# The tail's scores and the products with U, moved to a step's head between weighted values and main scores

## The chip, the cores and the metric

The kernel runs on one core of one Trainium2 chip. The metric is the device time of the program in microseconds; the time before is 1704.91 us, the median of three runs (1704.02, 1704.91, 1705.40). Everything is in fp32.

## The reference

Two blocks follow one another, over 8 batches of 8 heads, a sequence of 576 and a head dimension of 64.

```python
# attention in which each row keeps its 32 largest scores
scores = (1/8) * q @ k.T                       # 576 x 576 for each of 64 heads
kth = np.partition(scores, -32, axis=-1)[..., -32:-31]
scores = np.where(scores >= kth, scores, -1e9)
attn = exp(scores - max) / (sum + 1e-9)
x = (attn @ v), heads side by side             # (8, 576, 512)
# mixer: U is 576 x 32, V 32 x 576, w_ch1 512 x 2048, w_ch2 2048 x 512
h = x.T @ U @ V
u = x + h.T
out = u + np.maximum(u @ w_ch1, 0) @ w_ch2
```

## The kernel before

**Groups and tiles.** Two heads form a group g; there are 32 groups, four to a batch. The 576 rows of a group are four main tiles of 128 rows (both heads, scores of 2 x 576 columns) and a tail of 64 rows, in which both heads lie on top of each other: head 0 on partitions 0 to 63, head 1 on 64 to 127. The first four groups (ALONE) run a stage of their own, with five steps each. From group 4 on, a group takes four steps, and the fourth holds the last main tile and the tail together; these two-tile steps are where the change acts.

**What a tile goes through.** `scores` (product at L334) multiplies q and k into PSUM tiles `sc` of two banks each, of which two exist (pool ps_s). A main tile takes two `sc` tiles and fills 288 of the 512 columns of each bank; the tail takes one. ScalarE copies them to SBUF: L360 (into Ssb, main tiles of the later groups), L351 (into Stail, the tail). `fold` and `split` (L397, L399, L400, GpSimd and VectorE) split the scores into an upper and a lower half; VectorE finds the 32 largest with MAX8 and MATCH_REPLACE8 (L450 to L485). ScalarE and GpSimd mask the rest (L511, L514, L515), and ScalarE takes the exponential (L404). VectorE's 32 x 32 transposes (L541, into y), a write to DRAM (away) and a read back (L556, into PT, issued on ScalarE's queue) turn the weights around; tails and the earliest groups use TensorE for this (L577, L582). `values` multiplies with v into O (L602 for a tail, L615 and L618 for a main tile), three steps after the tile's own step; ScalarE copies O to XT (L627), or scales it into x (L610) for the tail.

**After a group.** `mixed` is a generator that a step's `fill` calls advance piece by piece. It transposes XT (L641), copies it to x (L645) and scales it on GpSimd (L646), waits for a number of `fill` calls, then multiplies with U (pT, L652), copies to Tb (L660) and computes two pieces of u transposed (up, L664 and L666, copied to uT at L674). After a batch's fourth group, its `mlp` joins the list of fillers.

**Fillers.** `mlp` yields after each matmul (mm, L701 with w1 and L719 with w2). `fill` first advances `mixed`, and then hands out as much of the first filler as a share worked out from the total allows; where the list is empty, the share is dropped, and that work is done after the attention is over. `tick` counts mm matmuls and starts, 12 of them later, the transposes and stores of finished results (L764, L766, and out_dram on SP's queue).

**Order.** All five engines are scheduled by hand: each engine executes its instructions in the order in which the program issues them. In a step n of the second stage:

```python
fill()
weighted(n - 3)                 # O of the step three back, tail first
for tile_ in tiles(n + 1):      # scores of the next step's main tile
    if tile_[1] < NT:
        scores(*tile_)
    fold(*tile_)
turn(); fill(); turn() ...
```

and at the very end of the step, after most of its fillers:

```python
if len(tiles(n + 2)) > 1:
    scores(*tiles(n + 2)[1])    # the tail's scores, two steps ahead
fill()
```

pT comes where the wait of five `fill` calls after L646 ends, in the middle of the step after the tail's O. PSUM has three pools of two buffers each: `sc`, `tp` (transposes, O, pT, up), and `mm`.

Of the kernel before, what the change touches and what calls it, by code (L numbers as in the profile page):

```python
# [8 lines left out]
F32 = mybir.dt.float32  # L9
# [17 lines left out]
def kernel(  # L27
# [28 lines left out]
    nc = tc.nc  # L56
    B, H, S, D = q.shape
    P = 128
# [4 lines left out]
    NT, TAIL = 4, 64  # L63
    MAIN = NT * P
    HALF = S // 2
    assert S == MAIN + TAIL and D == 64 and H % 2 == 0 and C == 512 and TOPK % 8 == 0
    NPAIR = H // 2
# [15 lines left out]
    attn = ctx.enter_context(tc.tile_pool(name="attn", bufs=2))  # L83
# [42 lines left out]
    def rows(t):  # L126
        return P if t < NT else TAIL

    def cols(t):
        return slice(t * P, t * P + rows(t))  # L130
# [4 lines left out]
    def half(h):  # L135
        return slice(h * D, (h + 1) * D)
# [97 lines left out]
    raw, qkTs, S2s, uTs, XTs, dens = {}, {}, {}, {}, {}, {}  # L234
    probs, PTs, folds, fronts_of = {}, {}, {}, {}
# [54 lines left out]
    def blocked(g):  # L290

        return g > NPAIR
# [23 lines left out]
            copy(qkT[:, i, 0:MAIN], tp.rearrange("p t n -> p (t n)"))  # L318
            yield

    def scores(g, t):

        qkT = qkTs[g]
        if t == NT and g >= NPAIR:
            S2 = attn.tile([P, S], F32, tag="Stail", name="Stail", bufs=1)
        else:
            S2 = attn.tile([P, 2 * (S + TAIL)], F32, tag="Ssb", name="Ssb", bufs=4)
        n = 2 if t < NT else 1  # L330
        probs[g, t] = S2
        S2s[g, t] = S2[:, 0 : n * S].rearrange("p (c n) -> p c n", c=n)
        def product(out, h, lo, hi):
            nc.tensor.matmul(  # L334
                out,
                lhsT=qkT[half(h), 0, cols(t)],
                rhs=qkT[half(h), 1, lo:hi],
                start=True,
                stop=True,
            )  # L340

        if t == NT:
            sc = ps_s.tile([P, 2, 512], F32, tag="sc", name="sc")
            for i in range(2):
                for h in range(2):
                    lo = i * HALF + (TAIL if h and blocked(g) else 0)
                    hi = min(lo + HALF, S)
                    product(sc[half(h), i, 0 : hi - lo], h, lo, hi)
                    if hi - lo < HALF:
                        product(sc[half(h), i, hi - lo : HALF], h, 0, TAIL)  # L350
            nc.scalar.copy(S2[:, 0:S].rearrange("p (i n) -> p i n", i=2), sc[:, :, 0:HALF])  # L351
            return
        scs = [ps_s.tile([P, 2, 512], F32, tag="sc", name="sc") for _ in range(2)]
        for i, sc in enumerate(scs):
            for h in range(2):
                part = 1 - i if h and blocked(g) else i
                product(sc[:, h, 0:HALF], h, part * HALF, (part + 1) * HALF)
        if blocked(g):
            for i, sc in enumerate(scs):
                nc.scalar.copy(ends_of(S2, i), sc[:, :, 0:HALF])  # L360
            fronts_of[g, t] = scs[0][:, :, 0:HALF]
            return

        main = S2.rearrange("p (h n) -> p h n", h=2)
        last = S2[:, MAIN : MAIN + 2 * TAIL].rearrange("p (h n) -> p h n", h=2)
        copy = nc.vector.tensor_copy if g + t == 0 else nc.scalar.copy
        copy(main[:, :, 0:HALF], scs[0][:, :, 0:HALF])  # L367
        nc.scalar.copy(main[:, :, HALF:MAIN], scs[1][:, :, 0 : MAIN - HALF])
        nc.scalar.copy(last, scs[1][:, :, MAIN - HALF : HALF])

    def ends_of(S2, i):

        parts = S2[:, 0 : 4 * HALF].rearrange("p (a n) -> p a n", a=4)
        return parts[:, 1:3] if i else parts[:, 0:4:3]
# [217 lines left out]
    def values(g, t):  # L592

        PT = PTs.pop((g, t))
        va, vd, vt = (a[g % NV] for a in (vas, vds, vts))
        O = ps_t.tile([P, P], F32, tag="tp", name="O")
        if t == NT:
            den, x = dens[g], xs[g % 2]
            if g not in inverted:
                inverse(g, 2 * NT if g == NPAIR - 1 else 0, 2 * NT + 1)  # L600
            for j in range(NT + 1):
                nc.tensor.matmul(  # L602
                    O,
                    lhsT=PT[:, j],
                    rhs=va[:, :, j, :] if j < NT else vt,
                    start=(j == 0),
                    stop=(j == NT),
                )
            for h in range(2):
                nc.scalar.mul(x[half(h), NT, half(h)], O[half(h), half(h)], den[half(h), 2 * NT :])  # L610
            return
        if shared(g, t):
            PT = PT.rearrange("p c n -> p (c n)")
            PT = PT.rearrange("p (a c j) -> p c a j", a=4, j=BLK)
        nc.tensor.matmul(O, lhsT=vd, rhs=PT[:, 2 * NT], start=True, stop=False)  # L615
        for j in range(NT):
            for h in range(2):
                nc.tensor.matmul(  # L618
                    O[half(h)],
                    lhsT=va[:, h, j, :],  # L620
                    rhs=PT[:, NT * h + j],
                    start=False,
                    stop=(j == NT - 1),
                )
        if t == 0:
            XTs[g] = attn.tile([P, MAIN], F32, tag="XT", name="XT", bufs=1)
        nc.scalar.copy(XTs[g][:, cols(t)], O)  # L627


    def mixed(g, wait, lag=0):  # L630

        for _ in range(lag):
            yield
        b, gi = divmod(g, NPAIR)
        if gi == 0:
            uTs[b] = mlpp.tile([P, NC, S], F32, tag="uT", name="uT")
        XT, den = XTs.pop(g), dens[g]
        X = xs[g % 2]
        tp = ps_t.tile([P, NT, P], F32, tag="tp", name="tp")
        for t in range(NT):  # L640
            nc.tensor.transpose(tp[:, t, :], XT[:, cols(t)], ident)  # L641
        X4 = X[:, 0:NT, :].rearrange("p t (h d) -> p t h d", h=2)
        tp4 = tp.rearrange("p t (h d) -> p t h d", h=2)
        den4 = den[:, 0 : 2 * NT].rearrange("p (t h) -> p t h ()", h=2).to_broadcast([P, NT, 2, D])
        nc.scalar.copy(X4, tp4)  # L645
        nc.gpsimd.tensor_tensor(X4, X4, den4, ALU.mult)  # L646
        for _ in range(wait):
            yield
        pT = ps_t.tile([P, P], F32, tag="tp", name="pT")
        for t in range(NT + 1):  # L650
            i = t % NT * R
            nc.tensor.matmul(  # L652
                pT[i : i + R, :],
                lhsT=U[:, t, :],
                rhs=X[:, t, :],
                start=(t < NT),
                stop=(0 < t),
            )
        Tb = mlpp.tile([P, P], F32, tag="Tb", name="Tb")
        nc.scalar.copy(Tb, pT)  # L660
        yield
        for chunks, (lo, hi) in zip(PARTS, SPAN):
            up = ps_t.tile([P, WIDE], F32, tag="tp", name="up")
            nc.tensor.matmul(up[:, 0 : hi - lo], lhsT=Tb, rhs=V[:, lo:hi], start=True, stop=False)  # L664
            for t in chunks:
                nc.tensor.matmul(  # L666
                    up[:, OFF[t] - lo : OFF[t] - lo + rows(t)],
                    lhsT=X[:, t, :],
                    rhs=ident if t < NT else ident2,
                    is_transpose=True if t < NT else None,  # L670
                    start=False,
                    stop=(t == chunks[-1]),
                )
            nc.scalar.copy(uTs[b][:, gi, lo:hi], up[:, 0 : hi - lo])  # L674
            yield
        if gi == NPAIR - 1:
            fillers.append(mlp(b))

    posts, ticks = [], 0

    def later(wait, job):

# [102 lines left out]
    STEPS = len(steps)  # L785
# [5 lines left out]
    fillers, mixing, due = [], [], 0.0  # L791
# [21 lines left out]
    def tiles(n):  # L813

        return steps[n] if 0 <= n < STEPS else []

    def weighted(m):

        for g, t in reversed(tiles(m)):
            values(g, t)  # L820
        if tiles(m)[-1][1] == NT:
            mixing.append(mixed(g, 5, 1 if m < STEPS - 1 else 0))

    def turn():

# [10 lines left out]
    t = 0  # L836
    for _ in prep(0):
        pass
    scores(0, 0)
    turning = ready = iter(())  # L840
    fronts = {}
    for n in range(STEPS + 2):
        if n < STEPS:
            g, t = steps[n][0]
# [6 lines left out]
        else:  # L851
            t = NT
# [71 lines left out]
        fill()  # L924
        if ALONE <= n - 3 <= STEPS - 3:
            weighted(n - 3)
        for tile_ in tiles(n + 1):
            if tile_[1] < NT:
                scores(*tile_)
            fold(*tile_)  # L930
        turn()
        fill()
# [37 lines left out]
            next_params(1)  # L970
        next(here, None)
        fill()
        if len(tiles(n + 2)) > 1:
            scores(*tiles(n + 2)[1])
        fill()
    while mixing or fillers:
        fill()
# [33 lines left out]
```

## Time and profile before

| | us |
|---|---|
| median of three runs | 1704.91 |
| lowest, highest | 1704.02, 1705.40 |
| the profiled execution | 1704.56 |
| its span, first to last instruction | 1702.7 |
| TensorE matmuls busy (PE) | 1606.2 |
| VectorE busy (DVE) | 1495.9 |
| ScalarE busy (ACT) | 993.5 |
| GpSimd busy (POOL) | 900.5 |

The profile shows one execution; times are counted from its first instruction. PE is TensorE's matmuls, PEld its weight loads. Matmuls overlap, and the busy time of PE counts a matmul until its results are out, so the start of the following one tells more than its length. Every fp32 matmul leaves two records. The chain of waits follows the work back from the last instruction: each piece in it was waited for by the next. A wait is put down to the instruction that came last. The first stage takes until about 233 us (the first O of group 4); the last O starts at 1557 us, and from then on only the last batch's mlp and its stores are left.

### The profile page before, as it was taken

How to read it: one execution, taken by the hardware profiler on the slowest of the kernel's cores; microseconds unless marked ns; L12 is line 12 of the kernel's file. 1: busy time of each engine (PE TensorE's matmuls, PEld its weight loads, DVE VectorE, ACT ScalarE, POOL GpSimd, SP SyncE). 2: the span in 40 equal slices, each digit the busy share in tenths (PEclk: the TensorE clock that was granted, in tenths of full speed). 3: DMA queues.
4: the chain of work that ended last, by engine and by line, in shares of the span. 5: the costliest groups of instructions: out<-in, count | busy, mean ns of one | idle time of the engine just before them, and what ended most of it. 6: DMA issues, size and time to landing. Idle time of an engine off the chain costs nothing.

```text
span 1702.7 us, 29005 instructions
## 1 busy us (share of the span) xinstructions
PE 1606.2 (94%) x9385; PEld 1210.6 (71%) x9385; DVE 1495.9 (88%) x4286; ACT 993.5 (58%) x2422; POOL 900.5 (53%) x695
## 2 busy tenths in 40 slices
PE   4566789999999999999999999999999999999999
PEld 2444556787677877788777877788777877788777
DVE  7999998999999999999999999999999999991000
ACT  4888778665556656565656556565656556563100
POOL 4778568656555555555555555555555555551000
PEclk7788899999999999999999999999999999999999
DMA  3322232255445454554544454554544454532010
GB/s 87 96 83 85 65 85 69 63 135 129 124 122 128 118 134 119 140 127 118 124 123 125 122 130 119 137 127 122 125 122 124 120 135 117 134 106 79 4 16 13
DMA packets 275832, 180.95 MB, mean 106 GB/s; under 512 B 173920, under 2 KB 260192, under 8 KB 275680
## 3 DMA queue, kind: packets, MB, share of 16 engines
q1 hardware_dynamic: 259648, 117.49, 29.8%
q10 hardware_dynamic: 16032, 61.61, 11.3%
q8 instruction: 74, 1.21, 0.3%
q14 instruction: 78, 0.64, 0.1%
HBM read 108.23 MB, written 70.78 MB: 105 GB/s over the span
## 4 chain that ended last, share of the span: by engine, by line
PE 85%; DVE 12%; ACT 1%; POOL 1%; issue 1%; DMA 0%; SPq 0%; DVEq 0%; POOLq 0%; ACTq 0%
PE mm L719 29%; PE mm L701 29%; PE sc L334 9%; PE O L618 7%; DVE m L485 5%; DVE upper L480 5%; PE up L664 2%; PE O L602 2%; DVE first L467 2%; PE O L615 1%; PE tp L577 1%; PE up L666 1%; PE pT L652 1%; PE tp L764 1%; PE tp L641 1%; DVE w L186 1%
## 5 line engine op out<-in xcount | busy, mean ns | idle before, releaser
L719 PE MATMUL mm<-hT,w 128*128 128x256 f32 (+1 forms) x2048 | 530.4, 409 | 0.0
L701 PE MATMUL mm<-uT,w 128*128 128x256 f32 (+1 forms) x2048 | 529.6, 410 | 0.0
L515 POOL TENSOR_TENSOR Ssb<-Ssb,E 128x576 f32<-128x576 f32 x243 | 339.7, 1417 | 275.7 <-ACT E L514 275.4
L701 PEld LDWEIGHTS mm<-uT,w 128*128 128x128 f32 x2048 | 379.2, 191 | 109.5 <-issue 8.4
L719 PEld LDWEIGHTS mm<-hT,w 128*128 128x128 f32 x2048 | 377.2, 190 | 104.4 <-issue 12.7
L485 DVE MAX8 m<-upper 128x8 f32<-128x304 f32 (+1 forms) x780 | 367.2, 512 | 0.7
L480 DVE MATCH_REPLACE8 upper<-m,upper 128x304 f32<-128x304 f32 (+1 forms) x520 | 259.7, 507 | 0.0
L397 POOL TENSOR_TENSOR lower<-Ssb 128x576 uint32<-128x576 uint32 x108 | 152.7, 1414 | 152.8 <-issue 100.1
L334 PE MATMUL sc<-qkT 64*128 64x288 f32 (+1 forms) x1334 | 210.2, 437 | 11.2 <-ACT Ssb L367 7.8
L404 ACT ACTIVATE Ssb<-Ssb,nmax 128x576 f32<-128x576 f32 x258 | 200.9, 780 | 18.6 <-POOL Ssb L491 9.7
L714 ACT ACTIVATE hT<-mm 128x320 f32<-128x320 f32 (+1 forms) x256 | 104.6, 409 | 181.9 <-PE mm L701 178.2
L400 POOL TENSOR_TENSOR lower<-lower,upper 128x576 uint32<-128x576 uint32 x108 | 152.7, 1414 | 100.3 <-DVE upper L399 95.2
L452 DVE MAX8 upper<-lower 128x8 f32<-128x288 f32 x432 | 172.3, 440 | 9.8 <-POOL lower L400 9.7
L514 ACT ACTIVATE E<-Ssb,least 128x576 f32<-128x576 f32 x243 | 176.2, 768 | 4.3
L334 PEld LDWEIGHTS sc<-qkT 64*128 64x128 f32 (+1 forms) x1334 | 115.6, 182 | 73.7 <-issue 29.0
L541 DVE STREAM_TRANSPOSE y<-Ssb 128x512 f32<-128x512 f32 (+1 forms) x312 | 154.8, 546 | 7.0 <-ACT Ssb L404 6.4
L360 ACT COPY Ssb<-sc 128x576 f32<-128x576 f32 x216 | 127.7, 644 | 36.6 <-PE sc L334 36.6
L618 PE MATMUL O<-PT,va 128*64 128x128 f32 x2048 | 144.5, 285 | 0.0
L731 DVE TENSOR_TENSOR oT<-uT,mm 128x320 f32<-128x320 f32 (+1 forms) x8 | 3.6, 454 | 144.6 <-PE mm L719 144.6
L618 PEld LDWEIGHTS O<-PT,va 128*64 128x64 f32 x2048 | 113.1, 140 | 16.1 <-issue 1.3
L399 DVE TENSOR_TENSOR upper<-sc,Ssb 128x576 f32<-128x576 f32 x108 | 80.3, 744 | 22.2 <-ACT Ssb L360 22.0
L480 DVE MATCH_REPLACE8 upper<-first,upper 128x304 f32<-128x304 f32 x216 | 97.7, 460 | 0.0
(111 smaller groups left out, 1893.3 us busy)
## 6 DMA issues: line engine op xcount, KB each, us to landing
away<-y SPq DMA_DIRECT2D x416, 144.0 KB, 2.5
PT<-away ACTq DMA_DIRECT2D x104, 576.0 KB, 3.8
raw<-in_moe_w_ch_dram SPq DMA_DIRECT2D x32, 512.0 KB, 3.8
va<-in_v_dram SPq DMA_DIRECT2D x64, 128.0 KB, 2.3
out_dram<-ob SPq DMA_DIRECT2D x57, 128.0 KB, 2.0
ld<-in_q_dram SPq DMA_DIRECT2D x108, 64.0 KB, 2.7
ld<-in_k_dram SPq DMA_DIRECT2D x108, 64.0 KB, 2.5
ld<-in_q_dram SPq DMA_DIRECT2D x108, 8.0 KB, 3.0
```

What stands on the lines that cost most here:

```text
L334: nc.tensor.matmul(out, lhsT=qkT[half(h), 0, cols(t)], rhs=qkT[half(h), 1, lo:hi], start=True, stop=True,)
L397: nc.gpsimd.tensor_tensor(bottom, a.bitcast(U32), b.bitcast(U32), ALU.add)
L404: nc.scalar.activation(E, chunk, AF.Exp, bias=nmax, scale=SCALE, accum_out=total)
L452: nc.vector.max(spot, lower)
L480: nc.vector.match_replace(nxt, ms[c], curs[c], NEG)
L485: nc.vector.max(ms[c], curs[c])
L514: nc.scalar.activation(gap, chunk, AF.Relu, bias=least[:, c : c + 1], scale=-WIDEN)
L515: nc.gpsimd.tensor_tensor(chunk, chunk, gap, ALU.subtract)
L541: nc.vector.transpose(y[:, :, i * NT : i * NT + c].rearrange("p r c j -> p c r j"), E2[:, a : a + c * P].rearrange("p (c r j) -> p c r j", ...
L618: nc.tensor.matmul(O[half(h)], lhsT=va[:, h, j, :], rhs=PT[:, NT * h + j], start=False, stop=(j == NT - 1),)
L701: nc.tensor.matmul(ph[:, 0:w], lhsT=w1[:, cc, f * P : (f + 1) * P], rhs=uT[:, cc, lo:hi], start=(cc == 0), stop=(cc == NC - 1),)
L719: nc.tensor.matmul(po[:, 0:w], lhsT=w2[:, f, c * P : (c + 1) * P], rhs=hTs[f][:, 0:w], start=(f == 0), stop=(f == NF - 1),)
```

## The change

Three things change in the second stage.

- The tail's scores are no longer issued at the end of the step two before, but at the head of the step before, after `weighted` and ahead of the main tile's scores of the same group. They take no `sc` tile of their own: in thirds of 192 columns they go into columns 288 to 479 of three of the four banks that the main tile's scores use. As the third at the end is cut at column 512 of the keys, and head 1's keys begin with the last 64 in the later groups, this is eight matmuls (four of 192 columns, two of 128, two of 64) where there were four or five.
- ScalarE copies them to Stail in two copies (384 and 192 columns), behind the copies of the main scores.
- `mixed` of groups 4 to 30 doesn't count five `fill` calls any more ahead of pT; it waits until the next step's head, where pT is issued right after `weighted` and ahead of the scores. up follows with the next two `fill` calls. The last group keeps its wait of five.

```diff
-    def scores(g, t):
+    def scores(g, t, tail=False):
...
-        if t == NT and g >= NPAIR:
-            S2 = attn.tile([P, S], F32, tag="Stail", name="Stail", bufs=1)
-        else:
-            S2 = attn.tile([P, 2 * (S + TAIL)], F32, tag="Ssb", name="Ssb", bufs=4)
+        S2 = attn.tile([P, 2 * (S + TAIL)], F32, tag="Ssb", name="Ssb", bufs=4)
...
         scs = [ps_s.tile([P, 2, 512], F32, tag="sc", name="sc") for _ in range(2)]
+        third = S // 3
+        spots = [sc[:, i, HALF : HALF + third] for sc, i in ((scs[0], 0), (scs[0], 1), (scs[1], 0))]
+        if tail:
+            rows_ = slice(MAIN, S)
+            for i, spot in enumerate(spots):
+                for h in range(2):
+                    lo, hi = i * third, min((i + 1) * third, MAIN)
+                    first_ = TAIL if h and blocked(g) else 0
+                    ranges = [(0, lo + first_, hi + first_)]
+                    if (i + 1) * third > MAIN:
+                        ranges.append((hi - lo, 0 if first_ else MAIN, TAIL if first_ else S))
+                    for to, lo, hi in ranges:
+                        nc.tensor.matmul(
+                            spot[half(h), to : to + hi - lo],
+                            lhsT=qkT[half(h), 0, rows_],
+                            rhs=qkT[half(h), 1, lo:hi],
+                            start=True,
+                            stop=True,
+                        )
...
             fronts_of[g, t] = scs[0][:, :, 0:HALF]
+            if tail:
+                tail_copies(g, scs, third)
             return
...
+    def tail_copies(g, scs, third):
+
+        S2 = attn.tile([P, S], F32, tag="Stail", name="Stail", bufs=1)
+        probs[g, NT] = S2
+        S2s[g, NT] = S2.rearrange("p (c n) -> p c n", c=1)
+        nc.scalar.copy(
+            S2[:, 0 : 2 * third].rearrange("p (i n) -> p i n", i=2), scs[0][:, :, HALF : HALF + third]
+        )
+        nc.scalar.copy(S2[:, 2 * third : S], scs[1][:, 0, HALF : HALF + third])
...
         nc.gpsimd.tensor_tensor(X4, X4, den4, ALU.mult)
-        for _ in range(wait):
-            yield
+        if wait is None:
+            waiting.append(g)
+            while g in waiting:
+                yield
+        else:
+            for _ in range(wait):
+                yield
...
-            mixing.append(mixed(g, 5, 1 if m < STEPS - 1 else 0))
+            mixing.append(mixed(g, None, 1) if m < STEPS - 1 else mixed(g, 5, 0))
...
             weighted(n - 3)
+            if waiting:
+                waiting.clear()
+                if next(mixing[0], True):
+                    mixing.pop(0)
         for tile_ in tiles(n + 1):
             if tile_[1] < NT:
-                scores(*tile_)
+                scores(*tile_, len(tiles(n + 1)) > 1)
             fold(*tile_)
...
-        if len(tiles(n + 2)) > 1:
-            scores(*tiles(n + 2)[1])
         fill()
```

More of the change, by code (lines that the diff above doesn't have):

```diff
@@ L369, in scores @@
         nc.scalar.copy(last, scs[1][:, :, MAIN - HALF : HALF])
+        if tail:
+            tail_copies(g, scs, third)
+    def tail_copies(g, scs, third):
[6 more added lines that the diff above has]
+        nc.scalar.copy(S2[:, 2 * third : S], scs[1][:, 0, HALF : HALF + third])
     def ends_of(S2, i):
@@ L677, in mixed @@
             fillers.append(mlp(b))
-    posts, ticks = [], 0
+    posts, ticks, waiting = [], 0, []
     def later(wait, job):
```

## The prediction

> **What bounds the kernel now.** I read the chain of waits first, then TensorE's waits, then the busy time by stretch, then the chain in order of time inside one group of four steps. TensorE holds the chain; the columns of the second fence are waits in total, times, longest.
>
> ```profile
> PE 85%; DVE 12%; ACT 1%; POOL 1%; issue 1%; DMA 0%; SPq 0%; DVEq 0%; POOLq 0%; ACTq 0%
> ```
>
> TensorE's waits from 258 us to the end:
>
> ```profile
> PE pT L652 <- POOL x L646: 3.0, 1, 3.0
> PE up L664 <- ACT Tb L660: 0.8, 2, 0.5
> PE tp L764 <- DVE oT L731: 0.5, 1, 0.5
> PE O L615 <- DMA PT<-away: 0.3, 1, 0.3
> ```
>
> In 1,445 us it waits under 5 us, 3 of them at one place. Only what TensorE itself takes can move the end much. VectorE is the next limit; in the table by stretch (busy us of PE, PEld, DVE, ACT, POOL; then the clock):
>
> ```profile
> 333.00:475.00 142.00, 138.66 (x846) 107.01 (x845) 141.72 (x430) 87.36 (x220) 80.91 (x62) 0.98 0.52 130
> ...
> 540.00:1500.00 960.00, 960.00 (x5741) 730.88 (x5742) 933.21 (x2817) 574.22 (x1409) 529.22 (x403) 1.00 0.49 125
> ```
>
> From 333 to 475 us VectorE has no slack (141.72 of 142); from 540 to 1500 it has 26.8 us in 960, 2.8%. Now one group, in the chain in order of time (start, length, what, records; every matmul leaves two records):
>
> ```profile
> 1029.73 5.38 PE mm L701 x20
> 1035.11 1.12 PE sc L334 x8
> 1036.24 1.81 PE mm L701 x6
> 1038.05 1.11 PE O L602 x10
> 1039.17 0.22 PE O L615 x2
> 1039.39 1.02 PE O L618 x16
> 1040.41 1.17 PE sc L334 x8
> 1041.58 1.27 PE mm L701 x4
> 1042.86 0.44 PE tp L641 x4
> 1043.30 4.31 PE mm L701 x16
> 1047.60 0.56 PE pT L652 x10
> 1048.16 1.27 PE mm L701 x4
> ```
>
> Undisturbed, an mm record takes 5.38/20 = 0.269 us. The six after the tail's scores (1035.11) take 1.81 where 6 x 0.269 = 1.61; the four after the main scores and the four after pT take 1.27 where they should take 1.08. So **every return to mm from a block that uses part of the array costs 0.19 to 0.20 us**, outside the block's own 1.12, 1.17 or 0.56. That is what this change can save.
>
> **The skill.** "TensorEngine Tiling (Array Packing)", section Key Properties, says that changing the tiling mode, not just the tile, drains TensorE. The trace agrees in effect: 0.19 to 0.20 us per return. "TensorE: Matmul & The Clock Gate", section LDWEIGHTS, prices a weight load at columns/1.2 ns, 107 ns for 128; about two loads no longer hidden would be that 0.2. The same page, section "The HAM clock gate", says that an idle window of about 3.4 us halves the clock. The trace agrees: TensorE idles 2.96 us before pT at 425.76, and the stretch 420 to 480 has a mean clock of 0.94 where its neighbours have 1.00: about 7 us at half speed, some 3.4 us lost.
>
> **The change, part by part.**
>
> *Order on TensorE.* Per group (28 in the second stage) returns from part-array blocks are now six: after four main scores, after the tail's scores, after pT. The tail's scores go between O (L618) and the main scores, both part-array already; pT likewise, one step later. The blocks keep their price, and each change into them stands where a change stood anyway (O to main scores). Four returns are left: **0.20 + 0.19 = 0.39 us per group saved**.
>
> *The tail's scores themselves.* Eight matmuls instead of four or five, of 192, 192, 128 and 64 columns per half instead of 288 and 288: the same 576 columns per half. The end phase has mm records of 256 columns at 27.64/128 = 0.216 and of 320 at 28.00/104 = 0.269: 0.053 per 64 columns, 0.004 fixed. Three more short records per half are 0.01 to 0.02 us, so 0.37 to 0.38 per group is left. Unseen in the trace: the change from the tail's 64x64 tiles to the main scores' 64x128. I take the same 0.2 as any other; it may cost nothing (another 0.2 per group gained), and at worst twice. Also unseen: whether the second half's 128 columns start while two matmuls of the first half stand ahead of them. pT runs four columns of the array side by side past such waits, so I take yes; if not, the last spot runs serially, 2 x (0.109 + 0.056) = 0.33 us per tail, against the gain.
>
> *ScalarE.* One copy of 576 columns (0.639) becomes 384 and 192. With the XT copy of 128 columns at 0.266, a column costs 0.83 ns and a copy 0.16 us: 0.48 + 0.32 = 0.80, that is 0.16 more per group, on an engine busy 574 of 960 us. Gone is its wait for the tail at the old place (35.8 us over 20 copies). Behind the new copies stand the exps L404, the PT transfer's issue L556 and the x copy L645, all up to 0.8 us later at that step. Near 1043 PT is issued at 1043.06 and, at 3.8 us to landing, there at 1046.9 for an O at 1051.5: covered by 4.6 us. Without that cover each 0.1 us late would cost 2.8 us. Tb's copy (0.27) now stands ahead of the two main-score copies, which wait for the scores behind pT anyway.
>
> *New waits of pT and up.* pT waits for x a step longer, so never. The first up waits for Tb and for XT's buffer: the main scores' 1.17 us lie between, against 0.27 for Tb plus its start. Covered.
>
> *POOL, SP.* Same instructions. In the built order some oT additions (0.87 us) change place with the subtraction L400; its reader L452 comes about 5 us later. Some stores of ob are issued behind four away transfers instead of ahead; nothing but ob's reuse waits for them. Both: nothing, at most 1 us where VectorE has no slack.
>
> *Filler.* In the built order the batch boundary near 422 us has no mm left until both ups are done, now a step later: two mm (4 x 0.269 = 1.08 us) move to the end.
>
> **The sum.** Savings count only where TensorE is not held by others. At the O's of 361.8, 406.9 and 452.6 us the PT transfer lands within 0.5 us of its use (at 452.6: issued 448.84, plus 3.8); its source is VectorE's 333 to 475 stretch. What is saved before 452.6 is lost but for what moves VectorE: its 2.4 us wait for the scores of 330.3 (L399 on the L360 copy) shrinks by 0.3 to 1.0, I take 0.5. The boundary at 422 keeps its idle time in another form: no pT to run, so TensorE waits for O's transfer (issued 422.70, landing about 426.4), and the half clock stays likely; it ends before the 452.6 point either way. After it lie 23 tails and 23 moved pTs: 23 x 0.38 = 8.7, less the 1.08 of filler: 7.6. With 0.5: 8.1 us. VectorE has 1.3 us of slack per group of 47.6 us; the change uses 0.4. Profiled execution: span 1702.7, time 1704.56; less 8.1 is 1696.5. The median shown is 0.35 above that execution, so I say **1696.6** (0.49% faster).
>
> **Rivals.**
> 1. *No drain between the tail's and the main scores*: 23 x 0.2 = 4.6 more, about 1692. For: both use 64 rows. Against: every change seen in the trace costs.
> 2. *VectorE or its transfers hold TensorE for longer*, for some groups past 452.6, as the slack of only 0.9 us at the O of 500.2 permits: half the gain, about 1700.5. Against: TensorE never waits from 540 to 1500.
> 3. *The change's packing doesn't pay*: the last spot serial, 23 x 0.33 = 7.6, and the gain is gone: 1704. For: three spots, the last in pieces.
> 4. *Slower: the first up stalls at every pT.* If ScalarE is inside its two E activations (2 x 0.77 us) when O ends, XT and then Tb come 2.1 us after O, against 0.56 + 1.17 of cover, and the main scores' copies slip too. A stall of s per group costs 27s; from 0.3 us the gain is gone, at 0.5 us it is 1704.6 - 8.1 + 13.5 = 1710. Against: 70 of 81 XT copies between 540 and 1500 us find ScalarE waiting, 1.1 us on average.
>
> **How the numbers follow.** Below 0.2% (3.4 us) a measurement of this kernel can't tell a change from none. Forecast 0.62 (gains of 5 to 11), rival 1 0.10, rival 2 0.13, rival 3 0.09, rival 4 0.06. Faster 0.62 + 0.10 + 0.13 = 0.85, same 0.09, slower 0.06. The range 1692.0 to 1702.0 takes in rivals 1 and 2 and part of 3; above it lies some 0.12, below it 0.05.
>
> **What would show it.** In the chain after the change, sc blocks of the tail stand straight after O L618 with a length near 1.13, followed by 1.17 for the main scores; pT stands before scores; mm runs after both old places show 0.269 per record throughout. Wrong: a new row of TensorE waits (up on Tb, sc or O on DMA) of more than 3 us; a tail block of 1.4 or more (rival 3) or a main block after it of 1.0 or less (rival 1); VectorE at 99% or more in 540 to 1500 (rival 2). More than 11 us gained or any loss means that the sum is wrong.

## The result and the profile after

The changed kernel takes 1700.36 us, median of 14 runs (1698.85 to 1702.07), against 1704.03 for the kernel before (14 runs, 1703.33 to 1705.62). The ratio is 0.9977, with a 95% interval from 0.9969 to 0.9985: faster by 0.23%, less than half of what was forecast, inside the range. The profiled execution took 1699.80 us with a span of 1698.0, against 1704.56 and 1702.7.

The chain in order of time inside one group of the changed kernel (start, length, what, records); the tail's scores have the line L363, the main scores L331, pT L687:

```profile
1025.90 7.00 PE mm L736 x26
1032.90 1.11 PE O L632 x10
1034.02 0.22 PE O L645 x2
1034.24 1.02 PE O L648 x16
1035.27 1.18 PE sc L363 x14
1036.45 1.17 PE sc L331 x8
1037.62 0.73 PE mm L736 x2
1038.35 0.44 PE tp L671 x4
1038.79 7.00 PE mm L736 x26
1045.79 0.22 PE O L645 x2
1046.01 1.02 PE O L648 x16
1047.04 0.55 PE pT L687 x10
1047.59 1.17 PE sc L331 x8
```

The order is the announced one. The two long mm runs take 7.00/26 = 0.269 us a record without a break: both returns are gone. What is left of them stands behind the main scores (two records of mm in 0.73 instead of 0.54). But the tail's block is 1.18 long, not 1.12.

TensorE's waits of the changed kernel from 258 us to the end (total, times, longest):

```profile
PE O L645 <- DMA PT<-away: 7.1, 4, 4.7
PE mm L736 <- ACT hT L749: 1.7, 1, 1.7
PE tp L607 <- ACT XT L657: 0.6, 1, 0.6
PE tp L799 <- DVE oT L766: 0.5, 1, 0.5
PE up L699 <- ACT Tb L695: 0.4, 1, 0.4
```

The 3.0 us of pT on x have gone, and O now waits 7.1 us for its transfers where it waited 0.3. The busy times by stretch say where these waits are not:

```profile
540.00:1500.00 960.00, 960.00 (x5907) 745.39 (x5903) 937.90 (x2831) 575.86 (x1441) 533.41 (x406) 1.00 0.50 126
```

TensorE is still without a gap from 540 to 1500 us, and VectorE has gone from 933.21 to 937.90: 22 us of slack are left. The O's (L618, now L648) that stand at 621.7 and 1386.7 us in the kernel before, 16 groups apart, come 3.1 and 8.5 us earlier: 0.34 us per group. That is steady all the way, and the rest was lost at the two ends of this stretch. The chain at the end of the attention:

```profile
1534.63 1.05 PE O L648 x16
1535.67 0.02 issue
1535.70 0.27 ACT XT L657
1535.96 0.66 ACT Ssb L434
1536.62 0.32 issue
1536.94 0.04 ACTq L586
1536.98 0.04 issue
1537.02 3.67 DMA PT<-away
1540.69 0.14 issue
1540.82 0.46 PE O L645 x2
```

The path leaves TensorE: O waits for PT, which is issued behind an exp on ScalarE. In the trace TensorE idles 1.52 us there, against 0.30 before. VectorE's last transposes ahead of this transfer (L541, now L571) have come forward by 6.0 us only, from 1537.16 to 1531.20, while TensorE reaches the place 7.0 us earlier.

### The profile page after: what moved, and what is told of

Read it like the earlier page. It is cut to its first block, busy times and chain, and to the rows that moved or that the text cites. A ratio compares the mean times of both kernels' runs of the same rounds, so it can differ in the third digit from the quotient of the medians.

```text
span 1698.0 us, 29412 instructions
## 1 busy us (share of the span) xinstructions
PE 1599.4 (94%) x9555; PEld 1224.4 (72%) x9555; DVE 1496.8 (88%) x4286; ACT 990.8 (58%) x2450; POOL 901.0 (53%) x695
## 4 chain that ended last, share of the span: by engine, by line
PE 77%; DVE 12%; POOL 4%; ACT 3%; DMA 1%; SPq 1%; issue 1%; ACTq 0%; DVEq 0%; POOLq 0%
PE mm L754 27%; PE mm L736 26%; PE sc L331 7%; PE O L648 6%; DVE m L515 4%; DVE upper L510 4%; PE up L699 2%; PE sc L363 2%; PE O L632 2%; PE O L645 1%; PE tp L607 1%; DVE first L497 1%; PE up L701 1%; PE pT L687 1%; POOL E L520 1%
## 5 line engine op out<-in xcount | busy, mean ns | idle before, releaser
L736 PE MATMUL mm<-uT,w 128*128 128x256 f32 (+1 forms) x2048 | 523.1, 409 | 1.7 <-ACT hT L749 1.7
L754 PE MATMUL mm<-hT,w 128*128 128x256 f32 (+1 forms) x2048 | 523.9, 408 | 0.0
L331 PE MATMUL sc<-qkT 64*128 64x288 f32 (+1 forms) x1056 | 177.2, 457 | 12.4 <-ACT Ssb L385 8.6
L571 DVE STREAM_TRANSPOSE y<-Ssb 128x512 f32<-128x512 f32 (+1 forms) x312 | 155.2, 545 | 8.8 <-ACT Ssb L434 8.8
L648 PE MATMUL O<-PT,va 128*64 128x128 f32 x2048 | 144.0, 284 | 0.0
L331 PEld LDWEIGHTS sc<-qkT 64*128 64x128 f32 (+1 forms) x1056 | 95.2, 196 | 52.8 <-issue 16.8
L648 PEld LDWEIGHTS O<-PT,va 128*64 128x64 f32 x2048 | 112.6, 140 | 16.3 <-issue 1.6
L801 ACT COPY ob<-tp 128x256 f32<-128x256 f32 x57 | 21.2, 372 | 130.7 <-PE tp L799 130.2
```

Source lines behind the costliest of these rows:

```text
L331: nc.tensor.matmul(out, lhsT=qkT[half(h), 0, cols(t)], rhs=qkT[half(h), 1, lo:hi], start=True, stop=True,)
L571: nc.vector.transpose(y[:, :, i * NT : i * NT + c].rearrange("p r c j -> p c r j"), E2[:, a : a + c * P].rearrange("p (c r j) -> p c r j", ...
L648: nc.tensor.matmul(O[half(h)], lhsT=va[:, h, j, :], rhs=PT[:, NT * h + j], start=False, stop=(j == NT - 1),)
L736: nc.tensor.matmul(ph[:, 0:w], lhsT=w1[:, cc, f * P : (f + 1) * P], rhs=uT[:, cc, lo:hi], start=(cc == 0), stop=(cc == NC - 1),)
L754: nc.tensor.matmul(po[:, 0:w], lhsT=w2[:, f, c * P : (c + 1) * P], rhs=hTs[f][:, 0:w], start=(f == 0), stop=(f == NF - 1),)
```

## The experiments

Each was timed beside the kernel before on the same chip. A place in a profile is named by the time at which its O (L618) starts in the kernel before.

**One half alone: the tail.** `mixed` as before, the rest of the change kept:

```diff
-            mixing.append(mixed(g, None, 1) if m < STEPS - 1 else mixed(g, 5, 0))
+            mixing.append(mixed(g, 5, 1 if m < STEPS - 1 else 0))
```

> Tail's scores at the step's head as in the change; pT keeps its wait of five fills. Theory A (every return of TensorE from a part-array block to the whole array costs 0.2 us, whatever else happens): the tail block measured 1.18 instead of 1.12 us in the profile of the changed kernel, so 0.20 - 0.055 = 0.14 us per group; what is saved before the O of 452 us is lost to VectorE, 23 groups are left: 3.3 us faster than before, less up to 1 us where the last PT transfers hold TensorE. mm records after the old place of the tail at 0.269 us each. Theory B (the returns cost nothing by themselves; the gain comes from ScalarE's lost wait for the tail and from pT): within 0.5 us of before.

Measured: 1703.28 against 1704.16, ratio 0.9994 (0.9986 to 1.0002). The time falls between the two forecasts and is not clear of no change; the rate is theory A's: between the O's of 500.5 and 1456.7 us, 20 groups, it gains 2.8 us, 0.14 per group. But at 500.5 us it is 1.2 us *later* than before. Before that point TensorE waits:

```profile
PE O L645 <- DMA PT<-away: 1.9, 3, 1.0
...
PE mm L736 <- ACT hT L749: 0.8, 1, 0.8
```

In the profile of this kernel the four away writes near 409 us are issued 0.3 us earlier than before, but the third and fourth take 4.4 us to land where they took 2.5 and 2.7, so PT is issued at 413.96 instead of 412.54. Nothing in the change alters these transfers, yet this is not one slow execution: in all six profiles of kernels with the tail's move these two writes take 3.9 to 4.4 us, in the three without it (the kernel before, and the experiments with pT alone and with a return more) 2.5 to 2.7. They go with the tail's move, then; how it brings them about was not tested.

**The other half alone: pT.** The kernel before, with the changed wait in `mixed` and the call behind `weighted`; `scores` untouched.

> pT at the next step's head as in the change; tail's scores at their old place in their old form. Theory A: 0.20 us per group, 23 groups after 452 us: 4.5, less 1.3 for three mm matmuls that the later start of the next batch moves behind the attention, less about 1.2 where the last PT transfers hold TensorE: 1.5 to 3 us faster than before. Idle at the batch boundary near 426 us about 4.7 instead of 3.3. Theory B (pT's place is what brought the whole gain of the change): 3.7 us faster or more, as the change.

Measured: 1702.67 against 1704.16, ratio 0.9990 (0.9982 to 0.9998), 1.5 us, the low end of theory A. Between the same two O's it gains 4.0 us in 20 groups, 0.20 per group. With the tail's 0.14 that is the 0.34 of the whole change: the two add up where TensorE is the bound.

**The third spot in alternation.**

```diff
...
-                    ranges = [(0, lo + first_, hi + first_)]
+                    pieces.append((0, h, 0, lo + first_, hi + first_))
...
-                        ranges.append((hi - lo, 0 if first_ else MAIN, TAIL if first_ else S))
-                    for to, lo, hi in ranges:
+                        pieces.append((1, h, hi - lo, 0 if first_ else MAIN, TAIL if first_ else S))
+                for _, h, to, lo, hi in sorted(pieces):
```

> The change, but in the third spot the two halves' matmuls alternate (128, 128, 64, 64 columns instead of 128, 64 of one half and then 128, 64 of the other). Theory A (the second half's second record waits behind the first half's short matmuls, 0.056 us per tail as the starts in the profile show): tail block 1.12 to 1.13 us instead of 1.18, and 23 x 0.055 = 1.3 us faster than the change, 5 us faster than before. Theory C (the block is longer because of the number of matmuls): block still 1.18, the time of the change.

Measured: 1699.43 against 1704.16, ratio 0.9971 (0.9960 to 0.9981); the chain of this kernel:

```profile
1034.97 1.13 PE sc L364 x16
1036.10 1.17 PE sc L331 x8
```

The block is at 1.13, in each of the 20 groups from 540 to 1500 us, where the changed kernel has 1.18 in each: theory A, and not the number of matmuls. In the starts of the changed kernel, the second half's second record of 128 columns begins 0.159 us after its first where 0.109 is usual, just 0.056 after the first half's. The gain over the change, 4.7 less 3.7 us, fits 1.3, but the two intervals overlap; the block's length carries the verdict, and the rate: between the O's of 500.5 and 1456.7 us this kernel gains 7.8 us in its profile and the changed one 6.8, 0.05 per group more.

**The batch boundary.** For group 7 alone the wait of five fills is kept:

```diff
-            mixing.append(mixed(g, None, 1) if m < STEPS - 1 else mixed(g, 5, 0))
+            mixing.append(mixed(g, 5, 0) if m == STEPS - 1 else mixed(g, 5 if g == 7 else None, 1))
```

> The change, but for group 7 alone, whose mixed stands at the batch boundary near 422 us, pT keeps its wait of five fills. Theory A (part of the gain is lost because no filler is left at this boundary: TensorE idles 4.7 us there instead of 3.3, and two mm of 1.08 us move to the end): idle there back to about 3.3, 1 to 2 us faster than the change. Theory D (VectorE sets the time up to 452 us whatever TensorE does): the O of 452 us where it was, within 0.5 us of the change but for the 1.08 us of filler.

Measured: 1699.02 against 1704.16, ratio 0.9969 (0.9957 to 0.9981), 5.1 us faster than before. TensorE's timeline at the boundary, of the changed kernel and then of this one (start, length, line, what, records, idle before):

```profile
426.51 0.77 PE L645 MATMUL O<-PT,vd 128*128 128x128 f32 x2 [4.67 <-DMA PT<-away]
```

```profile
425.55 1.04 PE L687 MATMUL pT<-x,U 128*32 128x128 f32 x10 [3.10 <-POOL x L676]
```

With pT there to be done, the gap is 3.1 us (and 0.35 before up), not 4.7. By the count of records this kernel has done as many mm up to the O of 621.7 us as the kernel before, where the changed one is two or three behind; it falls behind at the next batch boundary instead, after the point from which TensorE alone counts, where an mm that leaves the stage saves as much there as it costs at the end. That is theory A's direction, and the time is within its forecast, 1.3 us below the changed kernel's. But how much the boundary gave is not shown. At 500.5 us this kernel stands 0.3 us later than before; the changed one stands 0.6 earlier with three mm (1.6 us) undone, so 1.0 later with them counted. For this advantage of 0.7 there is a rival: from 420 to 440 us the mean granted clock of TensorE is 0.91 in this execution, and 0.83 in the other eight profiles, those with the same gap of 3 us among them. Over 20 us that is 1.6 us of work at full speed.

**Filler at the end.** In the first step after the last tile, the share of filler is multiplied by LATE, which is 1.6.

```diff
-            due += share * (LONG if len(tiles(n)) > 1 else 1) * (EARLY if n <= ALONE + BATCH + 2 else 1)
+            due += share * (LONG if len(tiles(n)) > 1 else 1) * (EARLY if n <= ALONE + BATCH + 2 else 1) * (LATE if n == STEPS else 1)
```

> The change, with six more mm matmuls handed out between the O's of 1534 and 1540 us (a factor of 1.6 on the share in the first step after the last tile), taken from the plain mlp that follows. Theory A (the 1.5 us that TensorE waits there for the last PT transfer are lost because VectorE, not TensorE, sets the end of the attention): that wait gone, 1.2 to 1.5 us faster than the change. Theory E (the wait only moves: O comes later, and the work behind it with it): within 0.4 us of the change.

Measured: 1697.78 against 1704.64, ratio 0.9961 (0.9949 to 0.9974). No wait is left at that O. The span is 2.0 us shorter than the changed kernel's (1696.0 against 1698.0), and the gain over the kernel before is 6.9 us against 3.7: more than theory A forecast. Theory E falls: work taken from the tail of the program fills the wait.

**The three mends together.** The diffs of the last three experiments in one kernel.

> The change with the alternating third spot, group 7's pT at its old place and the filler at the end, together. If the three losses are separate (1.0, 1.3 and 1.3 us): 3 to 4 us faster than the change, 7 to 8 us faster than before, near what the prediction had summed. If they are one loss seen three times: 1.5 us faster than the change.

Measured: **1696.74 against 1704.64, ratio 0.9953 (0.9939 to 0.9966)**: 7.9 us faster than before, the fastest kernel here, and within the forecast of 7 to 8 for separate losses. That is 4.2 us more than the change gains. But the three single gains over the change, 1.1, 1.5 and 3.2, would make 5.7, and the alternation and the filler alone 4.2. The O of 500.5 us is 0.9 us later than before in its profile, so the loss up to there isn't mended, and the boundary's part is not shown.

**A return more.** The kernel before with one mm of the filler between O and the main scores of every step:

```diff
             weighted(n - 3)
+            if fillers:
+                done = next(fillers[0], None)
+                if done is None:
+                    fillers.pop(0)
+                else:
+                    due -= done
```

> The kernel before, with one mm matmul of the filler taken ahead to stand between O and the main scores in every step of the second stage; nothing is added, the share is charged for it. Theory A: one return more per step; 91 steps after the O of 452 us at 0.20 us are 18 us slower than before, 17 to 20, and the mm records between O and scores show starts 0.37 us apart where 0.27 is undisturbed. Theory B (returns cost nothing by themselves, the mm that follow are merely late in the records): within 1 us of before.

Measured: 1727.49 against 1704.64, ratio 1.0134 (1.0120 to 1.0148). The chain inside a group:

```profile
1051.89 1.02 PE O L618 x16
1052.92 0.73 PE mm L701 x2
1053.65 1.17 PE sc L334 x8
1054.82 0.74 PE mm L701 x2
```

Two records of mm take 0.73 us where 0.54 is undisturbed, and the ones behind the scores pay again. From the O of 500.5 us to that of 1504.9, 84 steps, it loses 16.3 us: 0.194 per step. The other 6.6 us of the 22.9 were not expected: in the profile 3.8 are there by 500.5 us, so a loss of TensorE isn't hidden by VectorE there, and at the last O's it waits 2.1 us for PT and falls behind by more. Theory B is out: moving one matmul, with no work added, costs its return.

## Why the prediction was right or wrong

**Right: the bound and the mechanism.** TensorE's own time moves the end, and what was saved is the return from part-array blocks to the whole array. The forced return (0.194 per step) and pT alone (0.20 per group) show it by runs. The drain that the Trainium skill names (TensorEngine Tiling (Array Packing), Key Properties) agrees with this in effect. That the 0.2 is two weight loads no longer hidden, as the prediction computed, was argued and is not shown: a record of such a load for mm lasts 190 ns in the trace, where the prediction took 107.

**Right: no rival as stated.** Rival 1 is out: the main scores behind the tail's block take 1.17 us as ever, so the change between two kinds of part-array tile costs the usual. Rival 2 is out for the middle, with 22 us of slack. Rival 4 is out: the list of waits has up on Tb once, for 0.4. Rival 3 had the place right and the size wrong: 0.056 per tail and not 0.33.

**Wrong: the size, 8.1 against 4.7 us** (span against span; 3.7 by the medians). Four terms of the sum carry the difference:

| term | predicted | in the profile |
|---|---|---|
| per group, 23 groups | 0.38: 8.7 | 0.34: 7.8 |
| the O of 452.6 us | 0.5 earlier | 0.4 later |
| filler moved to the end | 1.08 | 1.3 (three mm) |
| the last PT transfers, and one up | 0 | 1.6 |
| sum | 8.1 | 4.5 (4.7 by the spans; 0.2 is left over) |

- *The tail's block.* Priced by columns at "0.01 to 0.02", it grew by 0.055 (1.125 to 1.180): a short matmul of one half stands ahead of the other half's. The step "pT runs past such waits, so I take yes" was half true; the experiment with alternation gave the 0.05 back.
- *The start.* That VectorE's wait at 332 us shrinks by 0.5 did not come true: its L399, now L429, waits 2.63 us where it waited 2.44, for the tail's copy. It starts 1.0 us earlier, but the first O of group 4 already stands 1.1 us earlier in this profile (231.55 against 232.68). Nor could TensorE use a gain there: it waits 4.67 us at the boundary and 1.72 for hT at 449. The prediction had the idle time at the boundary change form and took it as even.
- *The end.* The step that failed outright is a missing one. The claim that only what TensorE itself takes can move the end was checked from 540 to 1500 us. After the last scores VectorE works for 17 us without a wait for TensorE (1514.0 to 1531.2), and hands over through the away writes, ScalarE and a transfer of 3.7 us. The row of 0.3 us "O <- DMA PT" in the waits of before was that place: it said that nothing was to spare there.
- *Two or three mm.* The order of instructions had it right; from which matmul on it counts was off by one.
- *Small slips.* At the O of 406.9 us PT had landed 0.67 us ahead and not within 0.5. 1696.5 and 0.35 make 1696.8 and not 1696.6. On the clock, the trace shows the halving (16 records of O take 1.91 us at 429.9 and 1.02 elsewhere), but after an idle time of 2.96 us, which is shorter than the window of 3.4 that the prediction finds confirmed.

The parts costed at nothing held: ScalarE's two copies, the later PT at tail steps and the moved stores show in no wait of TensorE between 540 and 1500 us.

**Open:** what the late stand at 500 us is made of. Every kernel with the tail's move was late to use its savings there, and in every one the two away writes took at least 1.2 us longer to land. For the tail alone there is a second candidate at the boundary: its moved block of 1.18 us stands between O and the main scores, whose copies lead to x and to pT, and these copies start at 421.63 instead of 421.31 although O came 0.9 us earlier. Neither was tried by itself.

## What to carry to other kernels

Where TensorE is the bound, count its returns: matmuls that use part of the array belong next to each other. In this kernel each return avoided was worth the same 0.2 us, wherever it was. When a saving is spread over a long stretch, look at both ends of it, at the engine that sets the pace before and at the one that finishes last; here a wait of 0.3 us in the list of before marked a place with no slack. Work that is free to move, like fillers, should go where those waits will appear.

## What the runs showed beyond this

In the changed kernel VectorE's L429, which reads scores in PSUM, waits for the tail's copy from the same PSUM tile (waits of VectorE, 540 to 1500 us):

```profile
DVE upper L429 <- ACT Stail L396: 13.0, 16, 1.9
```

The prediction had these copies wait behind others, and nobody wait for them. VectorE had waited for the main scores' copies at this place before, and from 540 to 1500 us, where TensorE never waits, it costs nothing; whether it adds to the loss at the start (2.63 us at 331) or at the end (1.02 us at 1514) was not tried.
